# MLP matmuls that read and write their 512 columns 16 from one half and 16 from the other in turn, with the weights 192 bytes further on modulo 512

## The chip, the cores and the metric

The kernel runs on one core of one Trainium2 chip. The metric is the device time in microseconds (us) of that core for one execution of the whole program.

## What is computed

Banded attention is followed by a gated MLP. The attention has 8 batches, 8 heads, 576 tokens and head dimension 64; half of the heads see the last 32 tokens, the others every 32nd token before them. The heads' outputs, side by side, are the 512 inputs of each token's MLP, with 1024 hidden units and a convolution over three neighbouring tokens as the gate:

```python
scores = np.where(masks[None], scale * np.matmul(q, k.transpose(0, 1, 3, 2)), -1e9)
attn = softmax(scores)
x = np.matmul(attn, v).transpose(0, 2, 1, 3).reshape(B, S, H * D)   # 8, 576, 512
h = np.maximum(x @ w_in, 0.0)                  # 8, 576, 1024
conv = sum(conv_w[k] * hp[:, k:k + S] for k in range(3))   # hp: h with a zero token at both ends
out = (h * sigmoid(conv)) @ w_out              # 8, 576, 512
```

The MLP's weights come as float64; everything else is float32.

## The kernel before, in words

**Layout.** Features lie on the 128 partitions, tokens along the columns. The 8 x 576 = 4608 tokens are cut into nine groups of N = 512, whatever the batch. `xh` and `xl` hold the attention's output for two groups at a time, as a rounded value (high part) and what it lacks (low part), both in the matmul's 4-byte format fp32r. The weights are split likewise into `wih`, `wil` (first product) and `woh`, `wol` (second), and the gated hidden values into `gh`, `gl`. A product of two split numbers is the sum of three matmuls: high times high, low weights times high, high weights times low.

**First product** (`mm1`, the matmul in line 607). For each group and each of the 8 blocks of 128 hidden units, 4 input blocks times 3 matmuls add up in one PSUM bank of 512 columns. The weights are the stationary operand (128 x 128), the tokens the moving one (128 x 512). ScalarE takes the bank out with a relu; VectorE, ScalarE and GpSimd make the convolution and the gate (`conv_gate`) and split the result into `gh` and `gl`.

**Second product** (`mm2`, line 672). For each group and each of the 4 blocks of 128 outputs, 8 hidden blocks times 3 matmuls add up in a bank; ScalarE copies it out and SyncE's queue stores it. The helper `row` gives the 512 columns of hidden block f in `gh` or `gl`. In the last group the rows are 514 wide and the columns are cut in two, so that there each matmul has 256 or 258 columns instead of 512.

**Attention** (`probabilities`, `values`) runs 32 times, once for each batch and pair of heads, with small matmuls (L458 scores, L514 values, L449 masks) and a softmax on VectorE, ScalarE and GpSimd. In the first 60 us, besides, the weights are converted from float64 (`convert`, L411 to L421), and the first values' low parts are made by matmuls (L569) that read the columns of `xh` adjacent for one kind of heads and 32 columns apart for the other.

**Order.** Every operation is given to a planner (`Plan.op`) with an engine, an assumed duration, a due time and the keys that it reads and writes; the planner simulates the engines and writes the instructions out in the order that results. Line 607's and line 672's groups of three matmuls are one such operation each (assumed 0.683 and 0.697 us).

**Places in SBUF.** Tiles of the pool `const` lie behind one another in the order of their definition, each partition's bytes contiguous. Modulo 512 bytes the moving operands (`xh`, `xl`, `gh`, `gl`) and the weights (`wih`, `wil`, `woh`, `wol`) all start at 0 before the change; every slice that a full-width matmul reads starts a multiple of 512 further on.

Of the kernel before, what the change touches and what calls it, by code (L numbers as in the profile page):

```python
# [10 lines left out]
F32 = _mybir.dt.float32  # L11
F32R = _mybir.dt.float32r
BF16 = _mybir.dt.bfloat16
I32 = _mybir.dt.int32
# [6 lines left out]
P = 128  # L21
W = 32
# [42 lines left out]
class Plan:  # L65
# [6 lines left out]
    def op(self, engine, dur, at, fn, reads=(), writes=(), chain=(), table=None, lock=False, key=None):  # L72
        i = len(self.ops)
        deps = set(chain)
        for k in reads:
            if k in self.last_write:
                deps.add(self.last_write[k])
        for k in writes:
            deps.update(self.readers.get(k, ()))
            if k in self.last_write:  # L80
                deps.add(self.last_write[k])
        for k in reads:
            self.readers.setdefault(k, set()).add(i)
        for k in writes:
            self.last_write[k] = i
            self.readers[k] = set()
        deps.discard(i)
        self.ops.append((engine, dur, at, fn, deps, table, lock))
        return i
# [160 lines left out]
def tile_banded_attention_gated_mlp(ctx, tc, qkT, vw, w_in, conv, w_out, masks_in, picks_in, eye_in, out):  # L250
    nc = tc.nc
    B, NHP, _, S = qkT.shape
    S = (S - 32) // 2
    D, NSEG, NBLK = 64, 4, 5
    SEGS = [0, 5, 9, 14, 18]
    NF, NM = w_in.shape[0], w_out.shape[0] // 2
# [4 lines left out]
    N = 4 * P  # L261
# [6 lines left out]
    const = ctx.enter_context(tc.tile_pool(name="const", bufs=1))  # L268
    xh = const.tile([P, NC, 2 * N], F32R, name="xh")
    xl = const.tile([P, NC, 2 * N], F32R, name="xl")  # L270
    wih = const.tile([P, NC, FF], F32R, name="wih")
    wil = const.tile([P, NC, FF], F32R, name="wil")
    woh = const.tile([P, NF, DM], F32R, name="woh")
    wol = const.tile([P, NF, DM], F32R, name="wol")
    gh = const.tile([P, NF * (N + 2)], F32R, name="gh")
    eye = const.tile([P, P], F32, name="eye")
    eyer = const.tile([P, P], F32R, name="eyer")
    negr = const.tile([P, P], F32R, name="negr")
    picks = const.tile([P, 2, W], BF16, name="picks")
    small = const.tile([P, W], F32, name="small")  # L280
    cwords = const.tile([P, 3 * NF, 2], I32, name="cwords")
    gl = const.tile([P, NF * (N + 2)], F32R, name="gl")

    def attention_buffers(pool, i):
# [10 lines left out]
    mlp = ctx.enter_context(tc.tile_pool(name="mlp", bufs=1))  # L295
# [2 lines left out]
    misc = mlp.tile([P, 2 * NHB * L], F32, name="misc")  # L298
    hs = [misc[:, L * i:L * i + L] for i in range(NHB)]
    cs = [misc[:, L * (NHB + i):L * (NHB + i) + L] for i in range(NHB)]  # L300
    carry = mlp.tile([P, NF, 2], F32, name="carry")
    psum = ctx.enter_context(tc.tile_pool(name="psum", bufs=1, space=PSUM))
    psR = psum.tile([P, 2048], F32, name="r")
    psM = [psum.tile([P, 512], F32, name=f"m{i}") for i in range(NPM)]
# [1 line left out]
    words = [const.tile([P, 8 * P, 2], I32, name=f"ws{i}") for i in range(NWS)]  # L306
    wa = [const.tile([P, 8 * P], I32, name=f"wa{i}") for i in range(NWA)]
    wl = [const.tile([P, 8 * P], F32R, name=f"wl{i}") for i in range(NWL)]
    diag = const.tile([P, 2 * NBLK, W], F32, name="diag")
    cwa = const.tile([P, 3 * NF], I32, name="cwa")  # L310
    cwt = const.tile([P, 3 * NF], I32, name="cwt")

    def slot(n):
        return n % NB
# [277 lines left out]
    def chain():  # L592
        return [] if state["last"] is None else [state["last"]]

    def mm1(g, fl, at, early):
        banks = {}
        x0 = g % 2
        for f in fl:
            banks[f] = state["m"] % NPM
            state["m"] += 1  # L600
        for n, c in enumerate(HPS):
            for j, f in enumerate(fl):
                def products(n=n, c=c, f=f, ps=psM[banks[f]]):
                    fs = slice(f * P, f * P + P)
                    m = 0
                    for a, x in ((wih, xh), (wil, xh), (wih, xl)):
                        nc.tensor.matmul(ps, a[:, c, fs], x[:, c, N * x0:N * x0 + N], start=(n == 0 and m == 0),  # L607
                                         stop=(n == NC - 1 and m == 2))
                        m += 1
                state["last"] = op(T, 0.683, at + MM1_STEP * j, products,  # L610
                                   [("xh", c, x0), ("xl", c, x0), (("wi", f), "h"), (("wi", f), "l")],
                                   [("M", banks[f])], chain())
        for j, f in enumerate(fl):
            conv_gate(g, f, at + MM1_STEP * j, early, psM[banks[f]], ("M", banks[f]))
# [38 lines left out]
    def row(y, g, f):  # L653
        pitch = N if g < NG - 1 else N + 2
        return y[:, pitch * f:pitch * f + pitch]

    def mm2(g, m, at):
        ms = slice(m * P, m * P + P)
        oi = (state["h"] + (0, 1, 2, 2)[m]) % NHB
        o, ko = (hs[oi], [("h", oi), ("h0", oi)]) if m == 2 else (cs[oi], [("c", oi)])  # L660
        cuts = [0, N] if g < NG - 1 else [0, N // 2, N + 1]
        first, last = N * g - 1, m == NM - 1
        for t, (a0, z) in enumerate(zip(cuts, cuts[1:])):
            x = z - a0 & 1
            mi = state["m"] % NPM
            state["m"] += 1
            ps = psM[mi][:, x:z - a0 + x]
            for f in range(NF):
                def products(f=f, ps=psM[mi][:, :z - a0 + x], tok=slice(a0 - x, z)):
                    n = 0  # L670
                    for a, y in ((woh, gh), (wol, gh), (woh, gl)):
                        nc.tensor.matmul(ps, a[:, f, ms], row(y, g, f)[:, tok], start=(f == 0 and n == 0),  # L672
                                         stop=(f == NF - 1 and n == 2))
                        n += 1
                i = 2 * m + f // 4
                state["last"] = op(T, 0.697 if z - a0 == N else 0.36, at + 3 * t, products,
                                   [(("g", f), "h"), (("g", f), "l"), (("wo", i), "h"), (("wo", i), "l")], [("M", mi)], [])
            op(A, 0.59 if z - a0 == N else 0.38, at + 3 * t + 3, lambda ps=ps, a0=a0, z=z: nc.scalar.copy(o[:, a0:z], ps), [("M", mi)],  # L678
               ko)
            if g < NG - 1 or last:  # L680
                s = 1 if g == 0 else a0
                op(Q, 256 // len(cuts[1:]), at + 6, lambda s=s, z=z: nc.sync.dma_start(out=out[ms, first + s:first + z], in_=o[:, s:z]), ko, [])
        if g == NG - 1 and not last:
            op(Q, 256, at + 6, lambda: nc.sync.dma_start(out=out[ms, first:first + N + 1], in_=o[:, 0:N + 1]), ko, [])

    warm_ = const.tile([P, 256], BF16, name="warm")

    def warm_up():
        nc.vector.memset(warm_, 0.0)
# [3 lines left out]
    with tc.manual_schedule():  # L693
# [27 lines left out]
        for g in range(NG):  # L721
            early = g == 0
            t0 = GROUP_AT[g]
            for f in range(NF):
                if early and MAJOR:
                    if f % 2 == 0 and f < 2 * MAJOR:
                        mm1(g, [f, f + 1], t0 + MM1_STEP * f, early)
                    elif f >= 2 * MAJOR:
                        mm1(g, [f], t0 + MM1_STEP * f, early)
                else:  # L730
                    mm1(g, [f], t0 + MM1_STEP * f, early)
                if early and f % 2:
                    convert(w_out, W_OUT_AT[f // 2], "wo", f // 2)
            if g + 1 < B:
                for j in range(NHP):
                    n = (g + 1) * NHP + j + 1
                    load(n, ATTENTION_AT[g][j])
                    attention(n, ATTENTION_AT[g][j])
            for m in range(NM):
                mm2(g, m, t0 + MM2_AT[g] + MM2_STEP * m)  # L740
# [62 lines left out]
```

## Time and profile before

| | |
|---|---|
| median of 3 runs | 532.12 us (531.75 to 533.3) |
| the profiled execution | 531.87 us |
| its span, first to last instruction | 529.7 us |
| mean granted TensorE clock in the span | 0.986 |
| TensorE matmuls busy | 508.4 us, 96% of the span, 7352 instructions |
| TensorE weight loads busy | 409.9 us, 77% |
| VectorE, ScalarE, GpSimd busy | 362.3, 319.8, 118.3 us |
| DMA | 51.30 MB, mean 97 GB/s |

The busy time of an engine is the union of the times in which its instructions run. PE is TensorE with its matmuls; PEld are its weight loads, which run beside the matmuls. Matmuls are pipelined: the recorded durations of neighbours overlap, so that the distance from start to start says what one costs. A span is cut into 40 slices for the strips of digits; each digit is a share in tenths. The chain that ended last is followed back from the last instruction, at each step to what released it.

### The profile page before, as it was taken

How to read it: one execution, taken by the hardware profiler on the slowest of the kernel's cores; microseconds unless marked ns; L12 is line 12 of the kernel's file. 1: busy time of each engine (PE TensorE's matmuls, PEld its weight loads, DVE VectorE, ACT ScalarE, POOL GpSimd, SP SyncE). 2: the span in 40 equal slices, each digit the busy share in tenths (PEclk: the TensorE clock that was granted, in tenths of full speed). 3: DMA queues.
4: the chain of work that ended last, by engine and by line, in shares of the span. 5: the costliest groups of instructions: out<-in, count | busy, mean ns of one | idle time of the engine just before them, and what ended most of it. 6: DMA issues, size and time to landing. Idle time of an engine off the chain costs nothing.

```text
span 529.7 us, 16633 instructions
## 1 busy us (share of the span) xinstructions
PE 508.4 (96%) x7352; PEld 409.9 (77%) x7352; DVE 362.3 (68%) x639; ACT 319.8 (60%) x492; POOL 118.3 (22%) x197
## 2 busy tenths in 40 slices
PE   4787999999999999999999999999999999999997
PEld 3555677778877887788778877887788788888897
DVE  3977799866785668757975785688658845832940
ACT  2454776856584668656837675577547755733841
POOL 0111201532222112212231222222212221320220
PEclk9797999999999999999999999999999999999999
DMA  8656422352044303520334034303440001001001
GB/s 281 250 189 222 157 78 78 124 178 88 7 136 149 99 1 127 185 76 23 114 107 147 1 124 145 121 0 119 135 134 1 33 11 72 1 16 65 0 36 44
DMA packets 17639, 51.30 MB, mean 97 GB/s; under 512 B 2208, under 2 KB 3360, under 8 KB 17568
## 3 DMA queue, kind: packets, MB, share of 16 engines
q1 hardware_dynamic: 17568, 50.25, 28.1%
q8 instruction: 57, 0.93, 0.7%
q14 instruction: 14, 0.11, 0.1%
HBM read 40.80 MB, written 9.44 MB: 95 GB/s over the span
## 4 chain that ended last, share of the span: by engine, by line
PE 93%; ACT 2%; DVE 2%; DMA 1%; issue 1%; SPq 1%; DVEq 0%; ACTq 0%
PE m L672 39%; PE m L607 37%; PE r L514 6%; PE r L458 4%; PE m L411 2%; PE r L449 1%; DMA misc<-in_dram 1%; PE r L569 1%; PE m L412 0%; PE m L413 0%; ACT xh L549 0%; PE r L486 0%; DVE t L471 0%; DVE mx L470 0%; ACT wa L334 0%
## 5 line engine op out<-in xcount | busy, mean ns | idle before, releaser
L643 DVE SCALAR_TENSOR_TENSOR misc<-misc,cw 128x512 f32<-128x512 f32 (+29 forms) x256 | 126.8, 542 | 35.5 <-ACT misc L634 35.0
L672 PE MATMUL m<-gh,woh 128*128 128x512 f32 (+2 forms) x320 | 123.7, 387 | 0.0
L672 PE MATMUL m<-gh,wol 128*128 128x512 f32 (+2 forms) x320 | 118.2, 370 | 0.0
L672 PE MATMUL m<-gl,woh 128*128 128x512 f32 (+2 forms) x320 | 117.9, 368 | 0.0
L607 PE MATMUL m<-xh,wih 128*128 128x512 f32 x288 | 113.3, 393 | 0.0
L607 PE MATMUL m<-xh,wil 128*128 128x512 f32 x288 | 112.5, 391 | 0.0
L607 PE MATMUL m<-xl,wih 128*128 128x512 f32 x288 | 112.3, 390 | 0.0
L492 POOL TENSOR_TENSOR t<-t,sm 128x640 f32<-128x640 f32 x31 | 45.3, 1462 | 117.6 <-DVE sm L476 82.9
L672 PEld LDWEIGHTS m<-gh,woh 128*128 128x128 f32 x320 | 60.0, 188 | 12.2
L624 ACT ACTIVATE misc<-m 128x512 f32<-128x512 f32 x72 | 42.9, 596 | 42.8 <-PE m L607 41.0
L672 PEld LDWEIGHTS m<-gl,woh 128*128 128x128 f32 x320 | 60.2, 188 | 10.8
L672 PEld LDWEIGHTS m<-gh,wol 128*128 128x128 f32 x320 | 60.2, 188 | 8.4
L607 PEld LDWEIGHTS m<-xh,wih 128*128 128x128 f32 x288 | 54.2, 188 | 11.8 <-issue 0.2
L607 PEld LDWEIGHTS m<-xl,wih 128*128 128x128 f32 x288 | 54.2, 188 | 11.5
L607 PEld LDWEIGHTS m<-xh,wil 128*128 128x128 f32 x288 | 54.2, 188 | 11.0
L648 DVE TENSOR_TENSOR misc<-misc 128x512 f32<-128x512 f32 (+1 forms) x69 | 48.8, 708 | 12.6 <-ACT misc L646 12.4
L634 ACT ACTIVATE misc<-misc,cw 128x512 f32<-128x512 f32 (+1 forms) x70 | 50.5, 724 | 11.1 <-DVE gl L434 4.7
L646 ACT ACTIVATE misc<-misc 128x512 f32<-128x512 f32 (+1 forms) x72 | 44.6, 627 | 14.5 <-DVE misc L643 13.8
L431 ACT CAST gh<-misc 128x512 fp32r<-128x512 f32 (+1 forms) x72 | 44.2, 618 | 14.0 <-DVE misc L648 12.3
L678 ACT COPY misc<-m 128x512 f32<-128x512 f32 (+2 forms) x40 | 21.5, 545 | 47.5 <-PE m L672 47.0
L626 POOL COPY misc<-carry 128x2 f32<-128x2 f32 x64 | 18.9, 295 | 131.2 <-DVE misc L648 95.9
L470 DVE TENSOR_REDUCE mx<-r 128x10 f32<-128x640 f32 x32 | 26.2, 819 | 30.4 <-PE r L458 30.4
(84 smaller groups left out, 584.0 us busy)
## 6 DMA issues: line engine op xcount, KB each, us to landing
qk<-in_dram SPq DMA_DIRECT2D x32, 592.0 KB, 4.0
v<-in_dram SPq DMA_DIRECT2D x32, 384.0 KB, 3.6
ws<-in_dram SPq DMA_DIRECT2D x14, 512.0 KB, 5.1
out_dram<-misc SPq DMA_DIRECT2D x28, 256.0 KB, 3.1
misc<-in_dram SPq DMA_DIRECT2D x2, 512.0 KB, 6.3
out_dram<-misc SPq DMA_DIRECT2D x4, 255.5 KB, 3.4
out_dram<-misc SPq DMA_DIRECT2D x3, 256.5 KB, 2.0
masks<-in_dram SPq DMA_DIRECT2D x2, 160.0 KB, 2.6
```

Source lines behind the costliest of these rows:

```text
L431: op(A, ta, at, lambda: nc.scalar.copy(hi(), src), [skey], [(k, "h") for k in [key] + over])
L470: op(V, 0.826, at + offset[0], lambda: nc.vector.tensor_reduce(out=mx, in_=p3, axis=AX.X, op=ALU.max), ks, [("mx", i)])
L492: op(G, 1.28, at + offset[5], lambda: nc.gpsimd.tensor_tensor(out=t, in0=t, in1=sm.unsqueeze(2).to_broadcast([P, 2 * NBLK, 64]), op=ALU.mu ...
L514: nc.tensor.matmul(psV[64 * h:64 * h + 64, o:o + n_], v[W * c:W * c + W, h, j], tt[W * c:W * c + W, 64 * NBLK * h + a:64 * NBLK * h + z], ...
L607: nc.tensor.matmul(ps, a[:, c, fs], x[:, c, N * x0:N * x0 + N], start=(n == 0 and m == 0), stop=(n == NC - 1 and m == 2))
L624: op(A, 0.596, at + cg[2], lambda: nc.scalar.activation(out=h[:, 2:N + 2], in_=ps, func=AF.Relu), [kp], [("h", hi)])
L634: op(A, 0.725, at + cg[3], lambda: nc.scalar.activation(out=c_[:, :n], in_=h[:, 1:n + 1], func=AF.Copy, scale=w1), kh + ["cw"], [kc] + new)
L643: op(V, 0.11 + 0.00117 * (z - a), at + cg[4] + 0.4 * k, lambda k=k, wk=wk, a=a, z=z: nc.vector.scalar_tensor_tensor(out=c_[:, a:z], in0=h[ ...
L646: op(A, 0.63, at + cg[5], lambda: nc.scalar.activation(out=c_[:, :n], in_=c_[:, :n], func=AF.Sigmoid), [kc], [kc], table=1)
L648: op(ge, 0.69 if ge == V else 1.28, at + cg[6], lambda: (nc.vector if ge == V else nc.gpsimd).tensor_tensor(out=c_[:, :n], in0=h[:, 1:n + ...
L672: nc.tensor.matmul(ps, a[:, f, ms], row(y, g, f)[:, tok], start=(f == 0 and n == 0), stop=(f == NF - 1 and n == 2))
L678: op(A, 0.59 if z - a0 == N else 0.38, at + 3 * t + 3, lambda ps=ps, a0=a0, z=z: nc.scalar.copy(o[:, a0:z], ps), [("M", mi)], ko)
```

## The change

Two things are done. A helper `laced` turns a contiguous stretch of 512 columns into the order 0 to 15, 256 to 271, 16 to 31, 272 to 287 and so on. Both the moving operand and the PSUM output of the full-width matmuls are given in this order, so that each column's result lands where it did. Stretches under 512 columns stay as they are. And tiles of the pool `const` are defined in another order, which moves the four weight tiles to 192 modulo 512 bytes while the moving operands stay at 0.

```diff
     xh = const.tile([P, NC, 2 * N], F32R, name="xh")
     xl = const.tile([P, NC, 2 * N], F32R, name="xl")
+    cwords = const.tile([P, 3 * NF, 2], I32, name="cwords")
     wih = const.tile([P, NC, FF], F32R, name="wih")
     wil = const.tile([P, NC, FF], F32R, name="wil")
     woh = const.tile([P, NF, DM], F32R, name="woh")
     wol = const.tile([P, NF, DM], F32R, name="wol")
+    diag = const.tile([P, 2 * NBLK, W], F32, name="diag")
+    eye = const.tile([P, P], F32, name="eye")
+    carry = const.tile([P, NF, 2], F32, name="carry")
     gh = const.tile([P, NF * (N + 2)], F32R, name="gh")
-    eye = const.tile([P, P], F32, name="eye")
     eyer = const.tile([P, P], F32R, name="eyer")
     negr = const.tile([P, P], F32R, name="negr")
     picks = const.tile([P, 2, W], BF16, name="picks")
     small = const.tile([P, W], F32, name="small")
-    cwords = const.tile([P, 3 * NF, 2], I32, name="cwords")
+    warm_ = const.tile([P, 256], BF16, name="warm")
+    cwa = const.tile([P, 3 * NF], I32, name="cwa")
+    cwt = const.tile([P, 3 * NF], I32, name="cwt")
     gl = const.tile([P, NF * (N + 2)], F32R, name="gl")
...
+    def laced(y):
+        return y if y.shape[1] < N else y.rearrange("p (b a e) -> p a b e", b=2, e=16)
+
...
-                        nc.tensor.matmul(ps, a[:, c, fs], x[:, c, N * x0:N * x0 + N], start=(n == 0 and m == 0),
+                        nc.tensor.matmul(laced(ps), a[:, c, fs], laced(x[:, c, N * x0:N * x0 + N]), start=(n == 0 and m == 0),
                                          stop=(n == NC - 1 and m == 2))
...
-                        nc.tensor.matmul(ps, a[:, f, ms], row(y, g, f)[:, tok], start=(f == 0 and n == 0),
+                        nc.tensor.matmul(laced(ps), a[:, f, ms], laced(row(y, g, f)[:, tok]), start=(f == 0 and n == 0),
                                          stop=(f == NF - 1 and n == 2))
```

The old definitions of carry, diag, cwa, cwt and warm_ further down are taken out. The planner's operations, their assumed durations and their keys are the same.

More of the change, by code (lines that the diff above doesn't have):

```diff
@@ L300, in tile_banded_attention_gated_mlp @@
     cs = [misc[:, L * (NHB + i):L * (NHB + i) + L] for i in range(NHB)]
-    carry = mlp.tile([P, NF, 2], F32, name="carry")
     psum = ctx.enter_context(tc.tile_pool(name="psum", bufs=1, space=PSUM))
@@ L308, in tile_banded_attention_gated_mlp @@
     wl = [const.tile([P, 8 * P], F32R, name=f"wl{i}") for i in range(NWL)]
-    diag = const.tile([P, 2 * NBLK, W], F32, name="diag")
-    cwa = const.tile([P, 3 * NF], I32, name="cwa")
-    cwt = const.tile([P, 3 * NF], I32, name="cwt")
     def slot(n):
@@ L684, in mm2 @@
             op(Q, 256, at + 6, lambda: nc.sync.dma_start(out=out[ms, first:first + N + 1], in_=o[:, 0:N + 1]), ko, [])
-    warm_ = const.tile([P, 256], BF16, name="warm")
     def warm_up():
```

## The prediction

> **What bounds the kernel now.** I read the page first: the span, the busy shares, the slices, and the engine shares of the chain that ended last.
>
> ```profile
> span 529.7 us, 16633 instructions
> ...
> PE 508.4 (96%) x7352; PEld 409.9 (77%) x7352; DVE 362.3 (68%) x639; ACT 319.8 (60%) x492; POOL 118.3 (22%) x197
> ...
> PE   4787999999999999999999999999999999999997
> ...
> PEclk9797999999999999999999999999999999999999
> ...
> PE 93%; ACT 2%; DVE 2%; DMA 1%; issue 1%; SPq 1%; DVEq 0%; ACTq 0%
> ```
>
> TensorE is full from the fourth slice to the last but one, at the full granted clock, and 93% of the chain is its own work. The profiled execution took 531.87 us with a span of 529.7, so 2.17 us lie around the span; the median of the three runs shown, 532.12, is 0.25 above it. I make the sum against 531.87 and add 0.25 at the end.
>
> The second view is the table by stretches of time, for all engines and then for the two lines that the diff edits.
>
> ```profile
> 0.00:60.00 60.00, 42.22 (x1012) 30.71 (x1013) 42.56 (x65) 27.40 (x36) 8.95 (x13) 0.89 0.68 233
> 60.00:120.00 60.00, 60.00 (x943) 46.45 (x941) 50.42 (x76) 43.46 (x66) 15.42 (x20) 1.00 0.34 115
> ...
> 0.00:60.00 60.00, 4.70 (x16) 3.21 (x17) 0.89 0.68 233
> ...
> 503.26:529.70 26.44, 22.88 (x192) 22.67 (x191) 0.99 0.11 40
> ```
>
> The columns after the length are busy us with counts: PE, PEld, DVE, ACT, POOL in the first two rows, PE and PEld in the last two. Only 16 matmuls of the first MLP product (L607, third row) lie in the first 60 us, where TensorE waits for attention and for converted weights. In 60 to 120 us TensorE has no gap. The last row is the second product (L672) at the end: 192 matmuls of half width.
>
> A matmul's recorded duration does not say what one costs, since they overlap. So the third view is the time line, and the fourth the chain in order of time.
>
> ```profile
> 482.01 0.39 PE L607 MATMUL m<-xh,wih 128*128 128x512 f32 x1
> 482.24 0.39 PE L607 MATMUL m<-xh,wil 128*128 128x512 f32 x1
> ...
> 482.24 0.19 PEld L607 LDWEIGHTS m<-xl,wih 128*128 128x128 f32 x1
> ...
> 462.46 19.04 PE m L672 x84
> 481.50 21.76 PE m L607 x96
> 503.26 22.89 PE m L672 x192
> ```
>
> Each matmul records 0.39 us, and the next one starts 0.23 us later: the spacing is the cost. From the chain, 21.76/96 = 226.7 ns for L607 and 19.04/84 = 226.7 ns for L672, and 22.89/192 = 119.2 ns for the half-width ones (96 of 256 and 96 of 258 columns, mean 257). The two products read different tiles and have the same spacing, also where few other engines work, so it is TensorE's own. The next weight load starts with the matmul (both at 482.24) and lies beside it.
>
> Full and half width differ by 107.5 ns for 255 columns: 0.42 ns a column. 512 columns then take 215.8 ns, and **10.9 ns of each matmul are not columns**. At full width there are 3 x 8 x 4 x 8 = 768 matmuls of L672 (three products, eight blocks of FF, four of the output, eight groups) and 3 x 4 x 8 x 9 = 864 of L607 (three products, four blocks of the input, eight of FF, nine groups): 1632 in all, with 17.8 us of such time. This is all that an edit of the read order can win there.
>
> **The change part by part.** Every full-width MLP matmul reads 16 columns (64 bytes) from the first half of its 512, then 16 from the second, and writes PSUM in the same turn. The tiles are re-ordered: before, both operands start at 0 modulo 512 bytes; after it the moving ones at 0 and the weights at 192 (xh and xl are multiples of 512, cwords is 192; then 1280 + 512 + 64 of diag, eye and carry bring gh back to 0; 64 of gh's tail + 448 bring gl back). No instruction, wait, DMA or order of work is added or taken away; the planner's costs stay. Only the pace of each matmul can move.
>
> First term: the 10.9 ns. What could it be? The rows of weight loads by shape bear on it:
>
> ```profile
> L672 PEld LDWEIGHTS m<-gh,wol 128*128 128x128 f32 x320 | 60.2, 188 | 8.4
> ...
> L514 PEld LDWEIGHTS r<-tt,v 32*64 32x64 f32 x2688 | 32.4, 132 | 11.0 <-issue 5.7 <-DVE misc L643 2.1 <-DVE misc L648 1.4
> L458 PEld LDWEIGHTS r<-qk 64*32 64x32 f32 x2304 | 30.1, 108 | 1.2 <-issue 1.1
> ```
>
> A load of 32 columns takes 108 ns, of 64 132, of 128 188: (188-108)/96 = 0.83 ns a column, by the upper pair 0.88. That is **half the pace of the moving operand** (0.42); 128 columns are 106 ns. My supposition, which no row shows directly, is that the two reads of SBUF disturb each other when they stand at the same place modulo 512 bytes. Today the moving read goes through 512 bytes in 54 ns and the weight read in 106 ns, so the faster laps the slower once a load, and if it must follow it at half pace for some 20 ns, about 10 ns are lost. This is of the size of the 10.9, and like it a sum for each load, whatever the width. With 16 columns from each half in turn, the moving read goes through 512 bytes at half its pace, 0.83 ns for 4 bytes: the two march in step, 192 bytes apart, and never meet. Then the loss is gone.
>
> How many matmuls can gain? Where attention's products lie between, the neighbours are spaced otherwise:
>
> ```profile
> 171.47 0.39 PE L672 MATMUL m<-gl,woh 128*128 128x512 f32 x1
> 171.79 1.12 PE L514 MATMUL r<-tt,v 32*64 32x32 f32 x84
> 172.83 0.50 PE L607 MATMUL m<-xh,wih 128*128 128x512 f32 x1
> 173.18 0.40 PE L607 MATMUL m<-xh,wil 128*128 128x512 f32 x1
> ```
>
> The last before such a piece keeps TensorE 0.32 us and the first after it 0.35, not 0.227: something else is waited for. There are 64 pieces (32 of scores, 32 of values), some 56 past the first 60 us, so 112 such matmuls, and 16 lie in the first 60 us: 1632 - 128 = 1504 matmuls, times 10.9 ns = **-16.4 us**. Bounds: 0 if the 10.9 ns are a fixed price, -17.6 if 1616 gain.
>
> Second term: the broken runs. A full-width read now has 32 runs of 64 bytes. The nearest rows are those of L569, in whose first and third call here each column lies 128 bytes from the last, while in the second the columns are adjacent:
>
> ```profile
> 34.54 1.14 PE r L569 x8
> ...
> 42.44 1.12 PE r L569 x8
> ...
> 54.88 1.14 PE r L569 x8
> ```
>
> Eight matmuls with 576 columns take 0.02 us longer with 576 breaks: 0.035 ns each. 32 breaks cost 1.1 ns, times 1504 = **+1.7 us**. For the broken write no row exists, since all matmuls here write adjacent columns in their order. I bound a break, of read and write together, by 0 below (a broken pattern has the same columns to read and write as an adjacent one, so by itself it can't gain) and by one column of the slower pace, 0.83 ns, above, and take the 0.035 because it is the only measured break of TensorE's operand; the upper bound is a rival below.
>
> Third term: the 192 half-width matmuls at the end are not interleaved, but their weights move to 192 too. Under the same supposition the moving read now starts 48 columns behind the weight read and closes half a column for each of its own: it meets it after 96 columns, 40 ns, and follows for the other 66 ns of the load at half pace, losing 33 ns: +6.3 us. At best they lose their 10.9 ns: -2.1 us. PEld is busy for 22.67 of the 22.88 us of that stretch, so the load is near to setting the pace there, and a moving read that follows it costs; I take half of the upper bound, **+3.1 us**.
>
> Fourth term: what hides behind TensorE. At the new pace 60 us of its work become some 57 and DVE's 50.42 us of the fullest stretch still fit: 88%. I cost new waits at nothing; the cover is those 6 to 7 us in each 57, and without it each attention piece would wait about as long as DVE lags.
>
> Sum: 531.87 - 16.4 + 1.7 + 3.1 = 520.3, and with 0.25, **520.5 us**.
>
> **Rivals.** First, nothing changes: the 10.9 ns are a fixed price of changing weights. For it: two products with different tiles have the same 226.7. Against: both have their operands at 0 modulo 512, so they would collide alike. The time is 531.87 + 0.25, some 532. The Trainium skill ("TensorE: Matmul & The Clock Gate", section "Step-by-step: what each phase is for") says this rule: the moving operand and the weights come through two independent read ports, and loading the next weights takes no read bandwidth from the running matmul. By that rule the result is this rival's. The trace shows load and matmul side by side but leaves 10.9 ns without a name, so it neither bears the rule out nor refutes it.
>
> Second, on the slower side: each break of the 64-byte runs costs a column of the slower pace. Then a matmul gets 32 x 0.83 = 26.6 ns longer and 10.9 shorter: 1632 x 15.7 ns = +25.6 us, 557.7. The place is every L607 and full-width L672 matmul; it turns the sign from 10.9/32 = 0.34 ns a break. For it: a PSUM write out of order has no row here. Against: the reads of L569, ten times below that point. The Trainium skill ("PSUM — Partial Sum Buffer", section "Specifications (TRN2)") says that PSUM has 8-byte lines and that any non-contiguous pattern slows matmuls significantly. By its wording this rival holds; no run here shows such a write.
>
> Third, also slower: the reads march in step, but at the same place. If the weight read starts some 192 bytes' time after the matmul (48 x 0.83 = 40 ns), it is met at every column of the load: half of its 106 ns, 53, lost instead of 10.9, 1632 x 42 = +69 us, 601. Against it stand the starts above, which agree within 10 ns; against that, a record's start need not be the first read.
>
> **How the numbers follow.** The forecast has 0.70, nothing changes 0.12, dear breaks 0.13, the same place 0.05. A measurement of this kernel tells 0.3%, 1.6 us, from no change; faster is the forecast's 0.70, same 0.12, slower 0.18. The forecast's own low end is every gain and no cost: 531.87 - 17.6 - 2.1 = 512.2, so 512; its high end, with a tenth of the 16.4 left, is 530. The range takes in the first rival up to the highest run, 533, and so leaves 0.18 out.
>
> **What would show it.** Right: L607's 96 matmuls of the last group take 20.7 us in the chain, not 21.76 (215.8 ns each); L672's x84 piece 18.1; the last 192 take 22.9 to 29, longer than before; no waits of TensorE past 60 us. A spacing that stays at 227 with the same end is the first rival; one of 240 or more the second, of 265 or more the third. The forecast is wrong in its reason if the half-width matmuls gain as much as the full-width ones, since nothing but their weights' place has changed. It is wrong in its cover if the spacing falls and gaps before the attention lines (L449, L514) take the gain back.

## The result and the profile after

The changed kernel takes 551.32 us in the median (549.84 to 555.79, 6 runs) where the kernel before takes 531.90 (530.82 to 533.3, 6 runs beside them): a ratio of 1.0376, 95% interval 1.0338 to 1.0414. It is slower by 19.4 us. The profiled execution took 550.95 us, 19.1 more than that of before.

The page of the changed kernel, the lines that answer to those shown of before (span, busy times, TensorE's strip and granted clock, engine shares of the chain):

```profile
span 548.8 us, 16633 instructions
...
PE 527.7 (96%) x7352; PEld 415.1 (76%) x7352; DVE 363.5 (66%) x639; ACT 320.0 (58%) x492; POOL 116.3 (21%) x197
...
PE   4787999999999999999999999999999999999997
...
PEclk9997999999999999999999999999999999999999
...
PE 93%; ACT 2%; DVE 2%; DMA 1%; issue 1%; SPq 1%; DVEq 0%; ACTq 0%
```

Instruction counts and shares of the chain are those of before, and the granted clock differs in one early slice. PE is busy for 19.3 us longer, about what the span gained, and its weight loads for 5.2. DVE, ACT and POOL do what they did. Past the first 60 us TensorE waits for nothing, as before.

The time by stretches (PE, PEld, DVE, ACT, POOL busy with counts, then the clock) says where it is:

```profile
0.00:60.00 60.00, 42.45 (x1012) 30.94 (x1013) 42.70 (x65) 27.52 (x36) 8.95 (x13) 0.94 0.68 235
60.00:120.00 60.00, 60.00 (x935) 45.54 (x934) 48.99 (x75) 42.38 (x63) 14.66 (x19) 1.00 0.32 106
```

In the first 60 us 1012 matmuls run, as before. In the next 60 us TensorE is as full as before and gets 935 done instead of 943. The chain in order of time (start, length, what) shows the pace:

```profile
58.62 5.76 PE m L611 x24
...
479.02 20.16 PE m L676 x84
499.18 23.04 PE m L611 x96
522.22 23.00 PE m L676 x192
```

23.04/96, 20.16/84 and 5.76/24 are all 240.0 ns, where before had 226.7 in the last group. The half-width matmuls, which are not interleaved, take 23.00 us instead of 22.89. From the first dense piece (58.62, and 58.77 before) to the last matmul's end, 486.6 us have taken the place of 467.4: 19.2 us for some 1620 interleaved matmuls, 11.8 ns each. It is less than the 13.3 of the last group because the spacing before is not 226.7 everywhere: by the starts in its trace its six kinds of matmul (three products of `mm1`, three of `mm2`), where one stands next to another, have means from 226.8 to 229.6. After, all six have 240.0 or 240.1.

```profile
499.98 0.40 PE L611 MATMUL m<-xh,wil 128*128 128x512 f32 x1
500.22 0.40 PE L611 MATMUL m<-xl,wih 128*128 128x512 f32 x1
```

In the time line each matmul starts 0.24 us after the last. At the full clock that is one spacing for all, and no longer one that varies with the tiles.

### The profile page after: what moved, and what is told of

It is laid out like the page before. It is cut to its first block, busy times and chain, and to the rows that moved or that the text cites. A ratio compares the mean times of both kernels' runs of the same rounds, so it can differ in the third digit from the quotient of the medians.

```text
span 548.8 us, 16633 instructions
## 1 busy us (share of the span) xinstructions
PE 527.7 (96%) x7352; PEld 415.1 (76%) x7352; DVE 363.5 (66%) x639; ACT 320.0 (58%) x492; POOL 116.3 (21%) x197
## 4 chain that ended last, share of the span: by engine, by line
PE 93%; ACT 2%; DVE 2%; DMA 1%; issue 1%; SPq 1%; DVEq 0%; ACTq 0%
PE m L676 40%; PE m L611 38%; PE r L515 6%; PE r L459 4%; PE m L412 2%; PE r L450 1%; DMA misc<-in_dram 1%; PE r L570 1%; ACT xh L550 0%; PE r L487 0%; DVE t L472 0%; PE m L413 0%; DVE mx L471 0%; PE m L414 0%; ACT wa L335 0%
## 5 line engine op out<-in xcount | busy, mean ns | idle before, releaser
L676 PE MATMUL m<-gh,woh 128*128 128x512 f32 (+2 forms) x320 | 126.2, 394 | 0.0
L676 PE MATMUL m<-gl,woh 128*128 128x512 f32 (+2 forms) x320 | 121.1, 378 | 0.0
L676 PE MATMUL m<-gh,wol 128*128 128x512 f32 (+2 forms) x320 | 121.1, 378 | 0.0
L611 PE MATMUL m<-xh,wih 128*128 128x512 f32 x288 | 116.9, 406 | 0.0
L611 PE MATMUL m<-xh,wil 128*128 128x512 f32 x288 | 116.1, 403 | 0.0
L611 PE MATMUL m<-xl,wih 128*128 128x512 f32 x288 | 116.1, 403 | 0.0
L652 DVE TENSOR_TENSOR misc<-misc 128x512 f32<-128x512 f32 (+1 forms) x69 | 48.8, 709 | 15.9 <-ACT misc L650 15.7
```

What stands on the lines that cost most here:

```text
L611: nc.tensor.matmul(laced(ps), a[:, c, fs], laced(x[:, c, N * x0:N * x0 + N]), start=(n == 0 and m == 0), stop=(n == NC - 1 and m == 2))
L652: op(ge, 0.69 if ge == V else 1.28, at + cg[6], lambda: (nc.vector if ge == V else nc.gpsimd).tensor_tensor(out=c_[:, :n], in0=h[:, 1:n + ...
L676: nc.tensor.matmul(laced(ps), a[:, f, ms], laced(row(y, g, f)[:, tok]), start=(f == 0 and n == 0), stop=(f == NF - 1 and n == 2))
```

## The experiments

In each run I read the last dense pieces of the chain: 96 matmuls of the first product and 84 of the second, all at full width. Where only one time is given, the kernel ran once, for its profile. Places are counted modulo 512 bytes from the start of `xh`.

### Places or turns

`place_only` takes the interleaving out of the changed kernel; `lace_only` has the interleaving and the tiles in the order of before.

```diff
-nc.tensor.matmul(laced(ps), a[:, c, fs], laced(x[:, c, N * x0:N * x0 + N]), ...)
+nc.tensor.matmul(ps, a[:, c, fs], x[:, c, N * x0:N * x0 + N], ...)          # place_only, and so in mm2
```

> Only the places: weights at 192 modulo 512, moving operands at 0, all reads and writes adjacent as before. Theory A (each 64-byte run costs TensorE one beat of 0.83 ns, and the two reads collide by place): the full-width spacing leaves 227 ns, up to 33 ns more by the supposition of the prediction (260), so 532 to 580 us. Theory B (each run costs, the 10.9 ns before were a fixed price, place means nothing): 227 ns and 532 us. Theory C (place is what costs, runs are free): 240 ns and 551 us.

> Only the interleaving: 16 and 16 columns of read and write, all tiles where they were before, weights and moving operands at 0 modulo 512. Theory A (runs cost 26.7 ns a matmul, marching in step saves 13): 240 ns and 551 us unless the two reads then march at the same place, which would give over 260 ns. Theory B (runs cost 13 ns on top of a fixed price): 240 ns and 551 us. Theory C (place costs, runs are free): 227 ns and 532 us, or less.

The chain of `place_only`, then that of `lace_only`:

```profile
466.92 19.23 PE m L676 x84
486.15 21.97 PE m L611 x96
```

```profile
478.61 20.16 PE m L675 x84
498.77 23.04 PE m L610 x96
```

The turns (the interleaving) alone give 240.0 ns and 550.29 us (ratio 1.0342, 1.0309 to 1.0376), whatever the weights' place. The places alone give 228.9 ns and 535.19 us (1.0047, 1.0030 to 1.0065); in the profiled execution, whose span is 5.0 us longer than before's, only 2.1 of these lie behind the start of the 17th MLP matmul (444.8 us from there to the start of the last full-width one, against 442.7). Theory C is out. The expectation did not separate A from B here, except that A's larger loss by the places did not come.

### Read or write

Either only the moving operand or only the PSUM output is interleaved, so that the result's columns come out in another order.

```diff
-nc.tensor.matmul(laced(ps), a[:, c, fs], laced(x[:, c, ...]), ...)
+nc.tensor.matmul(ps, a[:, c, fs], laced(x[:, c, ...]), ...)      # lace_read
+nc.tensor.matmul(laced(ps), a[:, c, fs], x[:, c, ...], ...)      # lace_write; both so in mm2
```

> The changed kernel with the moving operand interleaved and the PSUM output written in adjacent order; the columns of the result come out in another order. If the broken read is what costs: 240 ns a full-width matmul and 551 us. If the broken write costs: 213 to 227 ns, 512 to 532 us.

> The changed kernel with the PSUM output interleaved and the moving operand read in adjacent order; the columns of the result come out in another order. If the broken write is what costs: 240 ns and 551 us. If the broken read costs: the spacing of the run with the places alone.

The chain of `lace_read` and that of `lace_write`:

```profile
478.13 20.16 PE m L676 x84
498.29 23.04 PE m L611 x96
```

```profile
464.61 19.23 PE m L676 x84
483.83 21.97 PE m L611 x96
```

The broken read has all of it: 240.0 ns and 550.05 us. The broken write is free: its pieces are to the hundredth those of `place_only`, which writes in order, and the kernel takes 534.54 us. The Trainium skill ("PSUM — Partial Sum Buffer", section "Specifications (TRN2)") says that any non-contiguous pattern slows matmuls significantly; with runs of 64 bytes this write does not, 228.9 against 228.9 ns.

### How long a run

With the tiles as before, the runs are 8, 32, 64 or 128 columns long, in the read and in the write. The cut is against `lace_only`.

```diff
-return y if y.shape[1] < N else y.rearrange("p (b a e) -> p a b e", b=2, e=16)
+return y if y.shape[1] < N else y.rearrange("p (b a e) -> p a b e", b=2, e=8)    # lace8; 32, 64, 128
```

> Tiles where they were before; 8 columns from one half and 8 from the other in turn, so 64 runs a matmul instead of 32. Theory A (each run costs 0.83 ns on a bare 213.3 ns, and the interleaving does away with what came on top before): 213.3 + 64 x 0.83 = 266.7 ns a full-width matmul. Theory B (each run costs 0.41 ns on top of the 226.7 of before): 253.3 ns. Theory D (the interleaving costs 13.3 ns whatever the length of a run): 240 ns.

> Tiles as before; 32 columns from each half in turn, 16 runs. Theory A: 213.3 + 16 x 0.83 = 226.7 ns, the time of before, 532 us. Theory B: 226.7 + 16 x 0.41 = 233.3 ns. Theory D: 240 ns.

> Tiles as before; 64 columns from each half in turn, 8 runs. Theory A: 213.3 + 8 x 0.83 = 220.0 ns, 521 us. If march in step is needed against the collisions and is lost at this length, 227 to 233 ns. Theory B: 226.7 + 8 x 0.41 = 230 ns, 537 us. Theory D: 240 ns.

> Tiles as before; 128 columns from each half in turn, 4 runs. Theory A: 213.3 + 4 x 0.83 = 216.7 ns, 516 us, or 227 to 230 if the collisions are back. Theory B: 226.7 + 4 x 0.41 = 228.3 ns, 535 us. Theory D: 240 ns.

The chains of `lace8`, `lace32`, `lace64` and `lace128`:

```profile
484.05 20.44 PE m L675 x84
504.49 23.36 PE m L610 x96
```

```profile
474.39 19.88 PE m L675 x84
494.27 22.72 PE m L610 x96
```

```profile
462.22 19.04 PE m L675 x84
481.26 21.76 PE m L610 x96
```

```profile
461.84 19.04 PE m L675 x84
480.88 21.76 PE m L610 x96
```

64 runs of 8 columns cost 243.3 ns (556.5 us), 32 runs of 16 240.0, 16 runs of 32 236.7 (545.59 us), 8 runs of 64 and 4 of 128 226.7 as without any. The last two take 532.29 us (ratio 0.9986, 0.9965 to 1.0006) and 531.97 (0.9986, 0.9964 to 1.0007): neither beats the kernel before. No theory fits. A price for each run (A, B) would double from 32 to 64 runs; it grows by 3.3 ns. A price for the turns as such (D) would not depend on the length. What holds is: runs of 64 columns and more are free, runs of 32 cost 10 ns, and the next two halvings only 3.3 more each.

### Where the weights stand, and how they are read

`places_a` and `places_b` put unused tiles between the weights and leave all reads adjacent. `weight_reads` and `still_weights` change which weight columns are loaded; the first product reads its tokens adjacent, the second 16 and 16. Theory E is that the two reads of SBUF, of the weights and of the moving operand, disturb each other; theory F is that the moving read alone sets the spacing.

```diff
+    pad0 = const.tile([P, 16], F32, name="pad0")       # places_a; 64 to 320 bytes ahead of each weight tile in the two runs
     wih = const.tile([P, NC, FF], F32R, name="wih")
...
-a[:, c, fs]
+a[:, c, P * f:P * f + 1].to_broadcast([P, P])          # still_weights, every MLP matmul
```

> Adjacent reads and writes as before; the weights moved against the moving operands by 64 (wih), 128 (wil), 256 (woh) and 384 bytes (wol) modulo 512. Theory E with a meeting once a load: the kinds differ by over 5 ns, and one of them falls below 220. Theory F: 227 ns in all kinds, 532 us.

> As the run before with 320 (wih), 448 (wil), 32 (woh) and 96 bytes (wol). Theory E: the kinds differ by over 5 ns, and one of them falls below 220. Theory F: 227 ns in all kinds, 532 us.

> Tiles as before. First product: adjacent moving reads as before; second: 16 and 16 columns in turn. In both, of each three matmuls the second loads one weight column 128 times over and the third every other column of a 256 wide stretch, so that part of the product is another one; the first loads 128 adjacent columns as ever. A matmul runs beside the load of the one behind it, so the spacing by kind shows the three loads. Theory E (the two reads of SBUF disturb each other): at least one kind moves away from 227 ns (first product) and from 240 ns (second) by 5 ns or more. Theory F (the moving read alone sets the spacing): 227 and 240 ns in all six kinds.

> Tiles as before. All MLP weight loads of 128 columns take one weight column 128 times, so both products are others than the kernel's; the moving read is adjacent in the first product and 16 and 16 in turn in the second. Theory E (the two reads disturb each other by where they stand): the first product leaves 227 ns, towards 215 if a still weight read is out of the way; the second leaves 240. Theory F (the moving read by itself): 227 and 240.

The chains of `places_a` and `places_b`:

```profile
466.69 19.43 PE m L677 x84
486.11 22.19 PE m L612 x96
```

```profile
468.17 19.51 PE m L677 x84
487.68 22.26 PE m L612 x96
```

The means by kind, from start to start in the trace, go from 228.5 to 235.7 ns in `places_a` and from 229.3 to 235.1 in `places_b`; the times are 536.70 us (ratio 1.0094, 1.0074 to 1.0115) and 538.29 (1.0136, 1.0106 to 1.0166). So the place of the weights does matter, by some 9 ns at most. The mean of the six kinds is lowest with 0, where the weights were before: 228.2 ns (226.8 to 229.6 by kind), against 229.3 with 192, 231.4 in `places_a` and 231.9 in `places_b`. But no kind comes near 220, which a meeting once a load would have given somewhere.

The chains of `weight_reads` and `still_weights`:

```profile
473.55 20.16 PE m L683 x84
493.70 22.40 PE m L618 x96
```

```profile
472.26 20.16 PE m L678 x84
492.42 22.24 PE m L613 x96
```

With 16 and 16 columns the spacing is 240.0 ns whichever weight columns are loaded. With adjacent reads it rises, to 233.3 and 231.7. A weight read that stands still does not free the moving one; it disturbs it a little more. Theory F holds for the interleaved read, theory E in a weak form for the adjacent one. The Trainium skill ("TensorE: Matmul & The Clock Gate", section "Step-by-step: what each phase is for") has two independent read ports and no loss of read bandwidth to the running matmul. The trace nearly agrees: the weights' place is worth at most 4% of a spacing, though not nothing.

### How much is loaded

The two matmuls with a low part load 72 and 100 weight columns, and the main one, now the last of three, 128. The very first matmul of each bank loads 128 too.

```diff
-nc.tensor.matmul(ps, a[:, c, fs], x[:, c, ...], ...)
+nc.tensor.matmul(ps[:wide(n, m)], a[:, c, P * f:P * f + wide(n, m)], x[:, c, ...], ...)   # 72, 100, 128
```

> Tiles as before, adjacent reads in the first product, 16 and 16 in turn in the second. The two matmuls that carry the low parts load only 72 and 100 weight columns, so those parts of the product are left out for the other outputs; the main one loads 128. By what a matmul runs beside, the kinds show loads of 72, 100 and 128 columns. Theory E (all time over 213.3 ns is lost while weights are loaded, in proportion): adjacent 220.8, 223.8, 226.7 ns; in turn 228.3, 234.2, 240.0. Theory F (the moving read alone, or a fixed price): 227 and 240 whatever is loaded.

The chain of `short_loads`:

```profile
468.85 20.16 PE m L678 x84
489.01 22.04 PE m L613 x96
```

240.0 ns again with 16 and 16, and 229.6 adjacent. By kind, the adjacent ones have 229.9 ns beside 72 columns being loaded (230.5 without those that lie beside the first load of a bank), 231.0 beside 100, 228.2 beside 128 (means from start to start). A loss in proportion to the load would have been 220.8, 223.8 and 226.7: theory E falls in this form, F holds.

### The moving read by itself

`still_reads` reads 16 columns 32 times over in the first product and one column 512 times in the second; `still_long` 64 columns 8 times and 256 columns twice; `two_runs` goes between two runs of 16.

```diff
-x[:, c, N * x0:N * x0 + N]
+x[:, c, N * x0:N * x0 + 16].unsqueeze(1).to_broadcast([P, 32, 16])     # still_reads, first product
-row(y, g, f)[:, tok]
+row(y, g, f)[:, 0:1].to_broadcast([P, N])                              # still_reads, second product
```

> Tiles as before. The first product reads its first 16 columns 32 times over, the second its first column 512 times, so both products are others than the kernel's. If the wrap to a next run costs by itself: 236 to 240 ns in the first product. If it is the jump to another place: 227 ns or less there. In the second product a read that never moves has no break: 227 ns if what came on top before is a fixed price, another value if it hangs on where the moving read stands.

> Tiles as before. The first product reads its first 64 columns 8 times over, the second its first 256 columns twice, so both are others than the kernel's. If a run of 64 hides its wrap as it did between two halves (lace64, 227 ns): 227 ns in both. If few places are cheaper than many, as one column was (215): below 227, the first product lower than the second.

> Tiles as before. The moving read goes between two runs of 16 columns only, 16 times each: 1024 bytes apart in the first product, 128 bytes apart in the second, so both products are others than the kernel's. If a jump costs by its distance modulo 512 (two runs at the same place get in each other's way): 240 ns in the first product, 227 to 235 in the second. If every jump costs alike: 240 in both. If a jump costs only into columns not read before: 227 or less in both.

The chains of `still_reads`, `still_long` and `two_runs`:

```profile
466.04 18.20 PE m L679 x84
484.24 23.22 PE m L614 x96
```

```profile
462.90 19.04 PE m L679 x84
481.94 21.76 PE m L614 x96
```

```profile
481.71 20.16 PE m L678 x84
501.86 23.23 PE m L613 x96
```

A run of 16 that repeats in place costs 23.22/96 = 241.9 ns: the jump is not needed, the wrap (from the end of one run to the start of the next) is enough. Going between two runs 1024 bytes apart costs 242.0, 128 bytes apart 240.0, so in these runs every wrap costs about alike. Runs of 64 and 256 in place cost 226.7, as `lace64` did between the halves. And a read that stays on one column comes down to 18.20/84 = 216.7 (215.0, 215.4 and 220.0 ns by kind), while weights of the usual form are loaded beside it. So the 7 to 12 ns by which an adjacent read lies above this are not a fixed price of changing weights. The Trainium skill ("TensorE: Matmul & The Clock Gate", section "Wait — 56ns, not 53.3ns?") gives 215.7 ns from start to start for 512 columns: only the read of one column reaches it, the adjacent 4-byte reads here take 226.7.

### Runs and jumps mixed

Each of the six kinds has a turn of its own: runs of 16 in 16, 8 or 4 parts, runs of 32 in 4 or 8 parts, runs of 4 in two.

```diff
+    def laced(y, e, b):
+        return y if y.shape[1] < N else y.rearrange("p (b a e) -> p a b e", b=b, e=e)
```

> Tiles and weights as before; the moving read and the write go in other turns, a different one for each of the six kinds. First product, runs of 16 columns: jumps of 128, 256 and 512 bytes between runs. Second product: runs of 32 columns with jumps of 512 and 256 bytes, and runs of 4 with jumps of 1024. If the length of a run alone decides: 240 ns for all three kinds of the first product, 236.6 for the two of 32, and 245 or more for the runs of 4. If it matters that the runs lie at the same place modulo 512 bytes: 227 ns with jumps of 128 and 256, 240 with 512.

The chain of `runs_and_jumps`:

```profile
478.20 20.16 PE m L675 x84
498.36 22.68 PE m L610 x96
```

By kind (means from start to start): runs of 16 with jumps of 128, 256 and 512 bytes 235.5, 234.7 and 238.6 ns; runs of 32 with 512 and 256 bytes 234.7 and 235.1; runs of 4 with 1024 bytes 249.3. Where short jumps cost 235, and not the 227 of the expectation, being at the same place modulo 512 is not what makes most of the cost. Nor does the run's length alone decide, which would have given 240 for all runs of 16. Whether the jump's length accounts for the rest stays inconclusive: here neighbours differ in kind, and `two_runs` has 240.0 with jumps of 128.

## Why the prediction was wrong

**What bounds the kernel**: right. TensorE's spacing alone moved, the span moved with it, and no engine or wait came in between. Two terms of the sum failed, and each accounts for about half of the distance from the forecast: the first for the 16.4 us of gain that did not come, the second for 17.5 us.

**The first term** (-16.4 us, the 10.9 ns of each matmul that are not columns): there is time of about this size above the columns, since a read of one column shows 215.0 to 220.0 ns by kind, near the 215.8 worked out. The supposed cause, and with it the gain, failed. The forecast supposed that the weight read is met once a load, from two paces that happen to be one to two. The runs that bear on it all speak against it: loads of 72 to 128 columns, weights that stay on one column, and ten places never brought the mean of a kind with adjacent reads below 226. That the two reads disturb each other in some other way is not excluded, as the weights' place is worth up to 9 ns. A march in step, 192 bytes apart, prevents nothing: interleaved, 192 and 0 bytes give the same 240.0.

**The second term** (+1.7 us, the broken runs) is the step that failed by size and turned the sign: 13.3 ns a matmul and not 1.1, 19.2 us over the whole kernel. It was priced from L569, 576 breaks in 0.02 us. The weight loads of the first two of those calls show why this row holds no price, the first call with broken reads, the second with adjacent ones (start, length, what):

```profile
34.53 0.97 PEld L569 LDWEIGHTS r<-xh,negr 128*128 128x128 f32 x8 [0.99 <-ACT xh L549]
...
42.44 0.97 PEld L569 LDWEIGHTS r<-xh,negr 128*128 128x128 f32 x8 [0.85 <-ACT xh L549]
```

The eight loads take 0.97 us in both, one every 111 ns, and the matmuls of 2 to 144 columns, each with a load of its own, follow them: from the first one's start to the last one's it is 0.80 us in both calls. The 0.02 us lie in the recorded end of the last matmul alone, though the cost of a matmul is read from start to start. What a break costs can hide under such a pace, so the piece does not show it. The upper bound, 0.83 ns a break, lay far nearer, with 0.42 measured in the mean, and the text took the lower because it was the only row. That the order of the PSUM write costs nothing lay at the term's lower bound.

**The third term** (+3.1 us for the half-width matmuls with moved weights): 0.1 us, 23.00 for 22.89. It hung on the same supposition.

**The fourth** (cover of the other engines) was not put to the test, as TensorE got slower.

**The rivals.** The second (dear breaks) had the place and the sign, and its spacing of 226.7 + 15.7 = 242.4 came near the 240.0. That was luck: its rule, a price for each break, fell with `lace8` and `lace32`. The first, a fixed price, is refuted by the read of one column, 215.0 to 220.0 under the same loads. The third needed 265. The upper end of the range took in only "nothing changes", though both slower rivals rested on operations without a row.

**What stays open**: why runs of 32 cost 10 ns and those of 16 and 8 only 3.3 more each, why runs of 64 hide it wholly, where the 7 to 12 ns between one column and adjacent columns go, and whether they are still in the 240.0 of a broken read. The runs say which of the operands makes the time, not by what part of the reader.

## What to carry to other kernels

Where a trace has no row for an edit that touches every instruction on the bounding engine, the range must reach to the far bound, however well a mechanism fits the size of a loss. Before a row is used as the price of an operation, look from start to start whether that operation sets the row's pace; in L569 the weight loads did. A mechanism that is built from a coincidence of two paces is cheap to try by one part: hold one of the two reads still, and see whether the loss goes. Give the 4-byte moving operand runs of at least 64 columns; the order in which PSUM is written was free in runs of 16.

## What the runs showed of the hardware

- Spacing of 512-column fp32r matmuls with a new 128-column weight load each, by how the moving operand is read: one column 215.0 to 220.0 ns, adjacent or runs of 64 and more 226.7 in the last group, runs of 32 236.7, of 16 240.0 to 242, of 8 243.3. In the run that mixes kinds: 234.7 to 238.6 for 16, 234.7 and 235.1 for 32, some 249 for 4. With runs of 32, 8 and 4 the write went in the same turns; its price was tried apart for 16 alone, where it is nothing.
- A moving run of 16 that repeats in place costs as much as one that jumps by 1024 bytes (241.9 and 242.0 ns).
- The place of the weights against the moving operand modulo 512 bytes moves an adjacent read's spacing by up to some 9 ns, and not one of 16 and 16 columns at the two places tried, 0 and 192 (240.0 ns in both).
- Weight loads of 128 columns behind one another, with matmuls of 2 to 144 columns, start every 111 ns, whether the matmuls read adjacent columns or columns 128 bytes apart.
